# Operand pieces, accumulator loads and the rounding of w3 in a fused attention and expert kernel

## The chip, the cores and the metric

The kernel runs on one core of a Trainium2 chip. The metric is the device time of one execution in microseconds (us), as the median over runs. Before the change it is 1210.27 us (three runs, 1209.18 to 1212.36).

## The reference

An attention over pooled keys and values gives x (2304 tokens, 512 wide); four experts, weighted by domain probabilities, follow; then a gated block with four weights:

```python
def _moe_ref(x, domain_probs, w1, w2):          # 4 experts, 512 -> 1024 -> 512
    p = domain_probs / (domain_probs.sum(-1, keepdims=True) + 1e-09)
    for e in range(E):
        h = np.maximum(x @ w1[e], 0.0)
        out += p[:, e:e + 1] * (h @ w2[e])

def _moe2_ref(x, w1, w2, w3, w_out):            # 512 -> 1024 -> 1024 -> 512
    a = x @ w1
    b = x @ w2
    h = a * b @ w3
    return (h @ w_out).astype(np.float32)
```

Here q, k, v and the experts' weights are float32; the four weights of the gated block come as float64 words, and the kernel rounds them to float32 on the chip.

## The kernel before

Every matrix product is made of three float32r matmuls on high and low parts (`mm3`, L169). The order of the work is written out by hand: the program text is the order on each engine and each DMA queue.

**Stages.** Attention and expert 0 come first. Then experts e = 1, 2, 3 run over the four batches of 576 tokens (`batch`, L1134); during the end of expert 3 the product of w3 and w_out begins, and the gated block follows. The change lies in experts 1 to 3.

**One batch** has two stages. The first is four calls of `hidden` (L1115), j = 0 to 3, each one `seven` (L913): a scheme with seven products of sums of blocks in place of eight. A product is 6 matmuls of 288 columns (so 42 a seven, 168 a batch). It takes its bank from a ring of eight PSUM banks (`bank_r`, L163); VectorE adds it to others on line 919, ScalarE and GpSimd make the hidden rows z from it (`sink`). The second stage multiplies z with w2: T tiles of 128 tokens (T = 4 in even positions n, 5 in odd ones), each 8 x 3 matmuls of 512 columns in a bank of its own. A "place" is one step of three matmuls; there are 8 T places. In the first 6 T the tiles take turns; then each tile has its last two, and at its last place `give` (L1186) has VectorE compute bank times probability plus the accumulator piece `ob` (L1188), which frees the bank. The piece is then stored to DRAM (L1190); in expert 3 it is transposed (`turn`, L1177; the first three tiles at once, the others during the next batch's sevens) and written as `turned`.

**What is done at places of the second stage** is a table (`act`, L1167 to L1224). Before the change:
- `fetch_operand` (L779) loads the next batch's operands (7 blocks x 4 rows of 288, high and low, from `kept_x` to `xo`) in eight column pieces of 4032 B a partition, at places 0 to 7, on ScalarE's DMA queue. All seven blocks of a row lie side by side in a piece.
- `load_ob` (L1172) loads the accumulator pieces at places 14 (m < 3) and 10, on ScalarE's queue; in the last batch of an expert on SP's queue, the fifth at place 4 T + 5. The first three use the tiles `c`, which the sevens use for their sums.
- `round_some` runs steps of the rounding: 6, 8, 7 of them in the second stages of the batches n = 0, 1, 2 at places spread over 1 to 6 T - 3; one more step falls into each of the sevens j = 1 and 3 from n = 1 on.

**Rounding** (L229 to L286). `step` keeps three loads in flight (`load`, L243, on SP), computes with five or six VectorE instructions and one GpSimd addition, and one step later hands the result to a sink, which stores it. There are 80 steps: 16 of w_out, 32 of w3, 32 of the gate weights. So w_out falls into e = 1, n = 0 and 1; w3 into e = 1, n = 2 to e = 2, n = 2; the gates into the rest. A step of w3 (`rounded_T`, L301) takes 128 rows and 256 columns; VectorE transposes it in blocks of 32 x 32 into one of two `turned` buffers (L309), and four DMAs of 32 partitions, 256 runs of 128 B each, write it transposed (L312).

Every DMA issue on a queue waits in order for what its tile needs, and for one earlier DMA that used the same semaphore.

Of the kernel before, what the change touches and what calls it, by code (L numbers as in the profile page):

```python
# [17 lines left out]
def fused_kernel(  # L18
# [159 lines left out]
    class Stream:  # L178
# [55 lines left out]
    class Rounding:  # L234
# [66 lines left out]
    def rounded_T(src, name):  # L301
# [3 lines left out]
        d = dpool.tile([n, rows], F32, tag=name, name=name)  # L305

        def sink(t, i, c):
            tt = dec.tile([P, HALF], F32, tag="turned", name="turned")
            nc.vector.transpose(tt, t)  # L309
            for m in range(P // 32):  # L310
                to = d[c:c + HALF, i * P + 32 * m:i * P + 32 * (m + 1)]
                nc.sync.dma_start(to.rearrange("(b i) j -> i b j", i=32),  # L312
                                  tt[32 * m:32 * (m + 1)].rearrange("i (b j) -> i b j", j=32))

        for i in range(rows // P):
            for c in range(0, n, HALF):
                rounding.add(words[i * P:(i + 1) * P, 2 * c:2 * (c + HALF)], lambda t, i=i, c=c: sink(t, i, c), "turn")
        return d

    with tc.manual_schedule():  # L320
# [456 lines left out]
        PIECES = 4  # L777
# [52 lines left out]
        def enter_experts():  # L830
            nonlocal dec
            x5[:] = [area(f"x5{t}", XT, F32, "x5" + t) for t in "hl"]
            dec = Places(din=row(x5[0], 0, 2048, 3), store=row(x5[1], 0, 2048, 3), turn=row(x5[1], 0, 2048, 2), turned=row(x5[1], 4096, 1024, 2))
            xuv = dict(x=Ring(plain, [2 * XB + 6 * HALF_ROW]), u=Ring(plain, [2 * XB + 7 * HALF_ROW]), v=Ring(p_area, [3 * HALF_ROW]))
            areas["x1l"] = area("x1l", XT, F32R, "edge")
            late["small"] = Places(c=c_ring, s=row(plain, 0, 2 * ROW, 2), turned=row(plain, 0, ROW, 2) + Ring(plain, [3 * ROW]),
                                   ob3=Ring(p_area, [320]), ob4=Ring(plain, [2 * ROW]), last=row(plain, 0, ROW, 4) + Ring(p_area, [320]),
# [75 lines left out]
        def seven(j, sink, meanwhile=None):  # L913
# [145 lines left out]
        def stream_last():  # L1059
            def add_w3(n):  # L1060
                _, (b,), fc = w_units[n]
                t0, rn = w3_blocks[b]
                stream.add([late["w3"][fc * P:(fc + 1) * P, t0 * P:(t0 + rn) * P]], (1, rn * P), rn)

            for k, fc in enumerate(turn_of):
# [3 lines left out]
                stream.add([late["wo"][fc]], (1, DM), dst)  # L1069
# [45 lines left out]
        def hidden(j, b, meanwhile=None):  # L1115
# [9 lines left out]
            seven(j, sink, meanwhile)  # L1125
# [8 lines left out]
        def batch(e, n, b):  # L1134
            last, end = n == B - 1, n == B - 1 and e == E - 1
            small = late["small"]
            for j in range(NJ):
# [22 lines left out]
            begin = b * S + -(b * S) % P  # L1160
# [253 lines left out]
```

## Time and profile before

| | us |
|---|---|
| median of 3 runs | 1210.27 (1209.18 to 1212.36) |
| the profiled execution | 1213.8 |
| its span, first to last instruction | 1212.1 |
| TensorE busy | 1165.7 (96%) |
| VectorE busy | 802.8 (66%) |
| GpSimd busy | 486.5 (40%) |
| ScalarE busy | 378.2 (31%) |
| mean granted TensorE clock | 0.989 |
| DMA of SP's queue | 168.91 MB, 45.5% of 16 engines |
| DMA of ScalarE's queue | 47.39 MB, 11.4% of 16 engines |

PE is TensorE, DVE VectorE, ACT ScalarE, POOL GpSimd, SP the queue of SyncE; a q behind an engine means its sequencer, which waits and issues DMAs. A clock of 1.00 is 2.4 GHz, 0.50 is 1.2 GHz. L12 is line 12 of the kernel. Names of tiles stand as out<-in.

### The profile page before, as it was taken

The page shows a single profiled execution, that of the slowest core. Times are in us where ns is not written, and L with a number is a line of the kernel's source. Part 1 is how long each engine was busy: PE and PEld are TensorE (multiplying, and loading weights), DVE is VectorE, ACT ScalarE, POOL GpSimd, SP SyncE. Part 2 cuts the span into 40 slices and gives each one's busy share as a digit, 9 for nine tenths or more (in the row PEclk, how much of TensorE's full clock was granted, in tenths as well). Part 3 has the DMA queues.
Part 4 walks back from the last instruction along what each step waited for, and adds up shares of the span by engine and source line. Part 5 has one row for each costly group of instructions (what it writes and reads, how often), then busy time and mean ns, then how long its engine had stood idle before and what let it go on. Part 6 is the DMA issues. An engine that isn't in the chain of part 4 may idle for free.

```text
span 1212.1 us, 19303 instructions
## 1 busy us (share of the span) xinstructions
PE 1165.7 (96%) x6812; PEld 1051.6 (87%) x6812; DVE 802.8 (66%) x1623; ACT 378.2 (31%) x688; POOL 486.5 (40%) x569
## 2 busy tenths in 40 slices
PE   7999999999999989999879999998999999999998
PEld 5798888999888888988869888797888999999997
DVE  6776543566585676766758667676687777785454
ACT  4443432346122133421304433031544332331010
POOL 6875222267262447633426664352300222251121
PEclk9999999999999999999899999998999999999999
DMA  8765524454846755467583654848467244845651
GB/s 201 194 158 136 163 99 149 151 217 169 284 152 211 219 145 171 140 188 228 134 259 109 193 192 118 278 123 235 144 178 263 103 161 167 320 171 206 224 181 44
DMA packets 209936, 217.52 MB, mean 179 GB/s; under 512 B 92720, under 2 KB 152880, under 8 KB 209840
## 3 DMA queue, kind: packets, MB, share of 16 engines
q1 hardware_dynamic: 193856, 168.91, 45.5%
q10 hardware_dynamic: 15984, 47.39, 11.4%
q8 instruction: 53, 0.87, 0.3%
q14 instruction: 43, 0.35, 0.1%
HBM read 144.41 MB, written 71.83 MB: 178 GB/s over the span
## 4 chain that ended last, share of the span: by engine, by line
PE 36%; DMA 8%; DVE 5%; POOL 3%; issue 2%; ACT 1%; SPq 0%; DVEq 0%; ACTq 0%; POOLq 0%
PE s L170 7%; PE s L172 7%; PE s L171 7%; PE g L171 5%; PE g L172 5%; PE g L170 5%; DMA w<-x5l 3%; DMA gate<-x5l 2%; POOL round L176 2%; DVE plain L919 1%; DVE x5l L277 1%; DMA plain<-acc 1%; DMA xo<-keptx 1%; DMA x5h<-in_moe_w_dram 1%; DVE x5l L273 1%
## 5 line engine op out<-in xcount | busy, mean ns | idle before, releaser
L176 POOL TENSOR_TENSOR round<-plain,round 128x576 fp32r<-128x576 f32 (+1 forms) x131 | 189.5, 1447 | 399.5 <-ACT round L175 303.3
L170 PE MATMUL s<-xo,wh 128*128 128x288 f32 x840 | 253.6, 302 | 30.7 <-DVE plain L1188 28.7
L172 PE MATMUL s<-xo,wh 128*128 128x288 f32 x840 | 251.7, 300 | 0.0
L171 PE MATMUL s<-xo,wl 128*128 128x288 f32 x840 | 251.0, 299 | 0.0
L170 PE MATMUL g<-w2l,round 128*128 128x512 f32 x540 | 211.6, 392 | 0.0
L172 PE MATMUL g<-w2h,round 128*128 128x512 f32 x540 | 210.9, 391 | 0.0
L171 PE MATMUL g<-w2h,round 128*128 128x512 f32 x540 | 210.8, 390 | 0.1
L170 PEld LDWEIGHTS s<-xo,wh 128*128 128x128 f32 x840 | 161.4, 192 | 35.1 <-DVE plain L1188 29.5
L919 DVE TENSOR_TENSOR plain<-s,plain 128x288 f32<-128x288 f32 x320 | 135.5, 452 | 73.7 <-PE s L172 40.0
L171 PEld LDWEIGHTS s<-xo,wl 128*128 128x128 f32 x840 | 161.2, 192 | 0.7
L172 PEld LDWEIGHTS s<-xo,wh 128*128 128x128 f32 x840 | 161.3, 192 | 0.0
L175 ACT ACTIVATE round<-plain 128x576 fp32r<-128x576 f32 (+1 forms) x135 | 90.9, 676 | 162.0 <-DVE plain L1263 159.0
L1122 ACT ACTIVATE plain<-plain 128x576 f32<-128x576 f32 x96 | 65.4, 682 | 183.0 <-DVE plain L919 182.6
L172 PEld LDWEIGHTS g<-w2h,round 128*128 128x128 f32 x540 | 101.3, 188 | 21.4
L170 PEld LDWEIGHTS g<-w2l,round 128*128 128x128 f32 x540 | 101.5, 188 | 20.8 <-issue 0.8
L171 PEld LDWEIGHTS g<-w2h,round 128*128 128x128 f32 x540 | 101.4, 188 | 20.1 <-DVE round L660 0.4
L279 POOL TENSOR_TENSOR x5l<-x5l 128x256 uint32<-128x256 uint32 x80 | 59.0, 737 | 143.2 <-DVE x5l L278 132.8
L921 ACT ACTIVATE plain<-s 128x288 f32<-128x288 f32 x80 | 31.9, 399 | 229.6 <-DMA plain<-acc 109.8
L919 DVE TENSOR_TENSOR plain<-s,pb 128x288 f32<-128x288 f32 x160 | 68.2, 455 | 19.2 <-PE s L172 7.4
L660 DVE SCALAR_TENSOR_TENSOR round<-g,round 128x384 fp32r<-128x384 f32 x48 | 26.6, 553 | 68.7 <-ACT round L659 68.4
L273 DVE TENSOR_SCALAR x5l<-x5h 128x256 uint32<-128x256 uint32 x80 | 39.4, 493 | 44.1 <-DMA gate<-x5l 13.0
L170 PE MATMUL g<-xl,round 128*128 128x384 f32 x192 | 66.6, 347 | 0.0
(249 smaller groups left out, 2247.4 us busy)
## 6 DMA issues: line engine op xcount, KB each, us to landing
xo<-keptx ACTq DMA_DIRECT2D x72, 504.0 KB
raw<-in_moe_w_dram SPq DMA_DIRECT2D x64, 256.0 KB
x5h<-in_moe_w_dram SPq DMA_DIRECT2D x64, 256.0 KB
keptx<-xo SPq DMA_DIRECT2D x16, 576.0 KB
plain<-acc ACTq DMA_DIRECT2D x30, 256.0 KB
acc<-plain SPq DMA_DIRECT2D x28, 256.0 KB
kept<-xo SPq DMA_DIRECT2D x12, 576.0 KB
xo<-kept SPq DMA_DIRECT2D x10, 576.0 KB
```

Of the source, the lines that this page charges most:

```text
L170: nc.tensor.matmul(ps, lh, rl, start=first, stop=False)
L171: nc.tensor.matmul(ps, ll, rh, start=False, stop=False)
L172: nc.tensor.matmul(ps, lh, rh, start=False, stop=last)
L175: nc.scalar.activation(hi, src, AF.Copy)
L176: (lo_eng or nc.vector).tensor_tensor(lo, src, hi.bitcast(F32), op=ALU.subtract)
L273: nc.vector.tensor_scalar(au, h, 0x7FFFFFFF, None, op0=ALU.bitwise_and)
L277: nc.vector.scalar_tensor_tensor(au, au, 3, bu, op0=ALU.logical_shift_left, op1=ALU.bitwise_xor)
L279: nc.gpsimd.tensor_tensor(au, au, bu, op=ALU.add)
L660: nc.vector.scalar_tensor_tensor(hl, ps, 0.0, hh.bitcast(F32), op0=ALU.max, op1=ALU.subtract)
L919: nc.vector.tensor_tensor(to, one, two, op=ALU.add)
L921: nc.scalar.activation(x, product(j, A11, B11), AF.Copy)
L1122: nc.scalar.activation(r, r, AF.Relu)
```

## The change

1. Operands: one piece for each of the seven blocks, all rows, high and low (4 runs of 1152 B a partition), on SP's queue. The first four are issued in the seven j = 3, behind its third to sixth product, each after its block's last use there; the other three at places 2, 6 and 10.
2. Accumulator pieces: loaded behind the seven j = 1, on SP's queue, into places of their own; in the last batches of experts 1 and 2 at places 5 to 9. In expert 3 all tiles are turned at once, the first three into `c` tiles.
3. w3 is rounded 32 rows at a time: four loads of 32 rows x 256 columns fill the 128 partitions, the transposed result goes out in one DMA of 1024 runs of 128 B. There are four `turned` buffers. The columns then lie in another order, so the rows of w_out are loaded in that order, in four pieces of 32 rows.
4. The rounding's places: 3 to 6 T - 6 instead of 1 to 6 T - 3.

```diff
@@ Stream.fill
                 if isinstance(src, list):
+                    step = P * a // len(src)
                     for j, part in enumerate(src):
-                        nc.sync.dma_start(r[:, j, :], part)
+                        nc.sync.dma_start(r[j * step:(j + 1) * step, 0], part)
@@ Rounding.load
+                if src.shape[0] < P:
+                    for n in range(0, P, 32):
+                        nc.sync.dma_start(view[n:n + 32], src[n // 32])
+                    self.loaded.append((r, sink, tag))
+                    continue
@@ rounded_T
-        d = dpool.tile([n, rows], F32, tag=name, name=name)
-        def sink(t, i, c):
+        d = dpool.tile([n // P, P, rows], F32, tag=name, name=name)
+        def sink(t, r):
             tt = dec.tile([P, HALF], F32, tag="turned", name="turned")
             nc.vector.transpose(tt, t)
-            for m in range(P // 32):
-                to = d[c:c + HALF, i * P + 32 * m:i * P + 32 * (m + 1)]
-                nc.sync.dma_start(to.rearrange("(b i) j -> i b j", i=32),
-                                  tt[32 * m:32 * (m + 1)].rearrange("i (b j) -> i b j", j=32))
-        for i in range(rows // P):
-            for c in range(0, n, HALF):
-                rounding.add(words[i * P:(i + 1) * P, 2 * c:2 * (c + HALF)], lambda t, i=i, c=c: sink(t, i, c), "turn")
+            to = d[:, :, r:r + 32].rearrange("b p j -> p b j")
+            nc.sync.dma_start(to, tt.rearrange("p (b j) -> p b j", j=32))
+        for r in range(0, rows, 32):
+            rounding.add(words[r:r + 32].rearrange("j (q c) -> q j c", q=P // 32), lambda t, r=r: sink(t, r), "turn")
@@ operands
-        def fetch_operand(b, kc, n):
-            step = 2 * XO // 4 // PIECES
-            cols = slice(n * step, (n + 1) * step)
-            nc.scalar.dma_start(whole(kc)[:, cols], kept_x[b][:, kc].rearrange("p n a s -> p (n a s)")[:, cols])
-            xo_next[kc] = x_places[kc]
+        USED = [B11, T2, T3, T4, T1, B21, B22]
+        def fetch_operand(b, n):
+            m = USED[n]
+            there = late["xo"].bitcast(F32).rearrange("p (g m s) -> p g m s", m=7, s=HB)[:, :, m]
+            nc.sync.dma_start(there, kept_x[b].rearrange("p k n m s -> p (k n) m s")[:, :, m])
+            if n == 0:
+                xo_next.update(enumerate(x_places))
@@ enter_experts: dec gets turned=row(x5[1], 4096, 1024, 2) + Ring(plain, [4 * ROW]) + Ring(p_area, [320 + ROW])
-            late["small"] = Places(..., turned=row(plain, 0, ROW, 2) + Ring(plain, [3 * ROW]),
-                                   ob3=Ring(p_area, [320]), ob4=Ring(plain, [2 * ROW]), last=row(plain, 0, ROW, 4) + Ring(p_area, [320]),
+            late["small"] = Places(..., turned=row(plain, 0, ROW, 2),
+                                   ob0=Ring(plain, [0]), ob1=Ring(plain, [ROW]), ob2=Ring(plain, [2 * ROW]), ob3=Ring(p_area, [320]),
+                                   ob4=Ring(plain, [3 * ROW]), ob5=Ring(x5[1], [2 * ROW]),
@@ seven
             add(v, product(j, S3, T3), u)
+            behind(0)
             add(c1[:, 0], product(j, A22, T4), v)
+            behind(1)
             p5 = product(j, S1, T1)
             add(c1[:, 1], p5, v)
             add(u, p5, u)
             sink(1, c1, None)
+            behind(2)
             add(c0[:, 0], product(j, A12, B21), x)
+            behind(3)
             add(c0[:, 1], product(j, S4, B22), u)
@@ stream_last
-                stream.add([late["wo"][fc]], (1, DM), dst)
+                rows = [divmod(256 * q + 32 * fc, P) for q in range(P // 32)]
+                stream.add([late["wo"][i][at:at + 32] for i, at in rows], (1, DM), dst)
@@ batch
+            def load_ob(m):
+                tag = "c" if last and not end and m < 3 else f"ob{m}"
+                if tag == "ob4" and last and not end:
+                    tag = "ob5"
+                obs[m] = small.tile([P, DM], F32, tag=tag, name="ob")
+                nc.sync.dma_start(obs[m], acc_d[:, tiles[m][0]])
             for j in range(NJ):
-                if j in (0, 2) and pieces_late:
-                    some.append(pieces_late.pop(0))
-                hidden(j, b, lambda: [f() for f in some])
+                kw = dict(behind=lambda i: fetch_operand(orders[e][n + 1], i)) if j == NJ - 1 and not last else {}
+                hidden(j, b, meanwhile=lambda: [f() for f in some], **kw)
+                if j == 1 and (end or not last):
+                    for m in range(T):
+                        load_ob(m)
-                tag = "last" if end else "c" if m < 3 else f"ob{m}"
-                (nc.sync if last else nc.scalar).dma_start(obs[m], acc_d[:, tiles[m][0]])
-                tt = late["small"].tile([P, DM], F32, tag="turned", name="tt")
+                tt = late["small"].tile([P, DM], F32, tag="c" if m < 3 and not end else "turned", name="tt")
-                elif m < 3 and not end:
+                elif not end:
                     turn(m)
-            for m in range(T):
-                act(14 if m < 3 else 10 if m == 3 or not last else 4 * T + 5, lambda m=m: load_ob(m))
             if not last:
-                for i in range(2 * PIECES):
-                    act(i, lambda i=i: fetch_operand(orders[e][n + 1], i // PIECES, i % PIECES))
+                for i in range(4, 7):
+                    act(4 * i - 14, lambda i=i: fetch_operand(orders[e][n + 1], i))
                 some = 8 if n == 1 else 6 + n // 2
                 for i in range(some):
-                    act(1 + (6 * T - 4) * i // (some - 1), lambda: round_some(1))
+                    act(3 + (6 * T - 9) * i // (some - 1), lambda: round_some(1))
             elif not end:
+                rounding.flush()
+                for m in range(T):
+                    act(5 + m, lambda m=m: load_ob(m))
```

## Rows read from the trace of the kernel before

**Rows 1.** The page's first part: busy us, share of the span and instructions by engine.
```profile
PE 1165.7 (96%) x6812; PEld 1051.6 (87%) x6812; DVE 802.8 (66%) x1623; ACT 378.2 (31%) x688; POOL 486.5 (40%) x569
```

**Rows 2.** The view of waits, whole span: us in total, times, longest.
```profile
PE s L170 <- DVE plain L1188: 29.0, 11, 6.4
...
PE s L170 <- DVE pb L919: 1.1, 2, 0.6
...
DVE x5l L309 <- DMA w<-x5l: 17.7, 11, 4.5
```

**Rows 3.** Busy times by stretch: four sevens each; then clock, DMA share, GB/s.
```profile
322.48:345.94 23.46, 22.86 (x169) 22.39 (x168) 17.33 (x35) 9.21 (x16) 11.12 (x12) 1.00 0.37 123
...
373.16:399.59 26.43, 24.11 (x170) 23.88 (x168) 17.88 (x39) 9.30 (x16) 11.70 (x14) 0.94 0.38 126
...
421.36:450.29 28.93, 24.11 (x170) 23.87 (x168) 22.10 (x52) 9.21 (x16) 13.09 (x15) 0.94 0.61 164
...
477.50:501.89 24.39, 22.56 (x169) 22.35 (x168) 12.03 (x28) 12.12 (x22) 16.43 (x17) 1.00 0.36 113
...
523.67:547.93 24.26, 23.03 (x170) 22.39 (x168) 18.43 (x43) 9.20 (x16) 11.14 (x13) 1.00 0.48 129
...
575.14:604.74 29.60, 24.41 (x170) 24.17 (x168) 22.37 (x55) 9.44 (x16) 14.19 (x17) 0.88 0.51 138
...
626.52:657.83 31.31, 24.91 (x169) 24.68 (x168) 22.46 (x53) 9.44 (x16) 14.00 (x17) 0.89 0.55 164
...
685.05:707.39 22.34, 22.34 (x169) 22.34 (x168) 12.09 (x28) 11.62 (x22) 14.96 (x16) 1.00 0.35 116
...
729.17:753.76 24.59, 23.39 (x170) 22.45 (x168) 19.27 (x39) 9.21 (x16) 10.42 (x12) 1.00 0.44 102
...
780.98:806.77 25.79, 23.40 (x170) 22.47 (x168) 20.45 (x43) 9.21 (x16) 10.79 (x13) 1.00 0.54 124
...
828.74:859.11 30.37, 25.02 (x170) 24.78 (x168) 24.69 (x56) 9.85 (x17) 13.62 (x16) 0.89 0.67 182
```

**Rows 4.** TensorE and VectorE in order of time, around 421 to 430.
```profile
429.55 0.40 PE L170 MATMUL s<-xo,wh 128*128 128x288 f32 x1 [4.82 <-DVE plain L1188]
...
421.21 0.45 DVE L309 STREAM_TRANSPOSE x5l<-x5l 128x256 f32<-128x256 f32 x1 [4.47 <-DMA w<-x5l]
...
428.74 1.41 DVE L1188 SCALAR_TENSOR_TENSOR plain<-g,pb,plain 128x512 f32<-128x512 f32 x2
```

**Rows 5.** Busy times by stretch: one second stage; two sevens j = 3.
```profile
399.59:421.36 21.77, 21.77 (x98) 18.02 (x97) 13.12 (x33) 2.64 (x4) 7.06 (x9) 1.00 0.91 280
...
541.90:547.93 6.03, 6.03 (x48) 6.03 (x46) 5.06 (x13) 3.96 (x7) 5.57 (x7) 1.00 0.01 1
...
800.50:806.77 6.27, 6.27 (x50) 6.27 (x48) 5.35 (x13) 4.17 (x7) 5.42 (x7) 1.00 0.39 84
```

**Rows 6.** DMA queues: packets, MB, share; 399.59 to 429.5, then the whole span.
```profile
q10 hardware_dynamic: 1728, 5.18, 48.4%
q1 hardware_dynamic: 8229, 2.53, 40.8%
...
q1 hardware_dynamic: 193856, 168.91, 45.5%
```

**Rows 7.** DMA issues on SP: ns min, median, max by line; a spell in time.
```profile
L312 SPq DMA_DIRECT2D w<-x5l x128: 302/442/1759, 397.7 to 626.3; - x128
...
L447 SPq DMA_DIRECT2D stxh<-in_q_dram x36: 311/430/4413, 16.2 to 146.2; - x36
...
L435 SPq DMA_DIRECT2D stxl<-in_q_dram x1: 578/578/578, 3.3 to 3.3; - x1
...
415.23 6.22 SPq L312 DMA_DIRECT2D w<-x5l  x4
```

**Rows 8.** VectorE in order of time: the first instruction of two steps.
```profile
631.60 0.29 DVE L273 TENSOR_SCALAR x5l<-x5h 128x256 uint32<-128x256 uint32 x1
...
633.54 0.28 DVE L273 TENSOR_SCALAR x5l<-x5h 128x256 uint32<-128x256 uint32 x1
```

More of the change, by code (lines that the diff above doesn't have):

```diff
@@ L304, in rounded_T @@
         words = src.bitcast(U32)
[L305 to L307 removed]
+        d = dpool.tile([n // P, P, rows], F32, tag=name, name=name)
+        assert n == P // 32 * HALF
+        def sink(t, r):
             tt = dec.tile([P, HALF], F32, tag="turned", name="turned")
             nc.vector.transpose(tt, t)
[L310 to L317 removed]
+            to = d[:, :, r:r + 32].rearrange("b p j -> p b j")
+            nc.sync.dma_start(to, tt.rearrange("p (b j) -> p b j", j=32))
+        for r in range(0, rows, 32):
+            rounding.add(words[r:r + 32].rearrange("j (q c) -> q j c", q=P // 32), lambda t, r=r: sink(t, r), "turn")
         return d
@@ L832, in enter_experts @@
             x5[:] = [area(f"x5{t}", XT, F32, "x5" + t) for t in "hl"]
-            dec = Places(din=row(x5[0], 0, 2048, 3), store=row(x5[1], 0, 2048, 3), turn=row(x5[1], 0, 2048, 2), turned=row(x5[1], 4096, 1024, 2))
+            dec = Places(din=row(x5[0], 0, 2048, 3), store=row(x5[1], 0, 2048, 3), turn=row(x5[1], 0, 2048, 2), turned=row(x5[1], 4096, 1024, 2) + Ring(plain, [4 * ROW]) + Ring(p_area, [320 + ROW]))
             xuv = dict(x=Ring(plain, [2 * XB + 6 * HALF_ROW]), u=Ring(plain, [2 * XB + 7 * HALF_ROW]), v=Ring(p_area, [3 * HALF_ROW]))
             areas["x1l"] = area("x1l", XT, F32R, "edge")
-            late["small"] = Places(c=c_ring, s=row(plain, 0, 2 * ROW, 2), turned=row(plain, 0, ROW, 2) + Ring(plain, [3 * ROW]),
-                                   ob3=Ring(p_area, [320]), ob4=Ring(plain, [2 * ROW]), last=row(plain, 0, ROW, 4) + Ring(p_area, [320]),
+            late["small"] = Places(c=c_ring, s=row(plain, 0, 2 * ROW, 2), turned=row(plain, 0, ROW, 2),
+                                   ob0=Ring(plain, [0]), ob1=Ring(plain, [ROW]), ob2=Ring(plain, [2 * ROW]), ob3=Ring(p_area, [320]),
+                                   ob4=Ring(plain, [3 * ROW]), ob5=Ring(x5[1], [2 * ROW]),
                                    xr=Ring(x5[1], [0]), t=Ring(x5[0], [0]), **xuv)
@@ L911, in settle, with seven @@
                 pending.pop(0)()
-        def seven(j, sink, meanwhile=None):
+        def seven(j, sink, meanwhile=None, behind=lambda n: None):
             x, u, v = (late["small"].tile([P, HB], F32, tag=t, name=t, bufs=1) for t in "xuv")
@@ L1062, in add_w3 @@
                 t0, rn = w3_blocks[b]
-                stream.add([late["w3"][fc * P:(fc + 1) * P, t0 * P:(t0 + rn) * P]], (1, rn * P), rn)
+                stream.add([late["w3"][fc, :, t0 * P:(t0 + rn) * P]], (1, rn * P), rn)
             for k, fc in enumerate(turn_of):
@@ L1113, in take_x, with hidden @@
             xo_next.clear()
-        def hidden(j, b, meanwhile=None):
+        def hidden(j, b, **kw):
             at = (0, P - S % P) if b % 2 else (S - S % P, 0)
@@ L1124, in sink @@
                 nc.gpsimd.tensor_copy(edge_of(fc)[:, :, at[1]:at[1] + S % P], t[:, :, at[0]:at[0] + S % P])
-            seven(j, sink, meanwhile)
+            seven(j, sink, **kw)
         def round_some(n):
@@ L1136, in batch @@
             small = late["small"]
+            begin = b * S + -(b * S) % P
+            tiles = [(begin // P + m, lambda fc, off=begin - b * S + m * P: z_t[fc][:, :, off:off + P]) for m in range(S // P)]
+            if n % 2:
+                tiles.insert(0, ((b // 2 * 2 + 1) * S // P, edge_of))
+            T = len(tiles)
+            obs = {}
+            def load_ob(m):
[4 more added lines that the diff above has]
+                nc.sync.dma_start(obs[m], acc_d[:, tiles[m][0]])
             for j in range(NJ):
@@ L1159, in batch @@
                 stream.fill()
-            begin = b * S + -(b * S) % P
-            tiles = [(begin // P + m, lambda fc, off=begin - b * S + m * P: z_t[fc][:, :, off:off + P]) for m in range(S // P)]
-            if n % 2:
-                tiles.insert(0, ((b // 2 * 2 + 1) * S // P, edge_of))
-            T = len(tiles)
             banks = [bank_r("g2") for _ in tiles]
-            obs = {}
             acts = {}
@@ L1170, in act @@
                 acts.setdefault(at, []).append(f)
-            def load_ob(m):
-                tag = "last" if end else "c" if m < 3 else f"ob{m}"
-                obs[m] = small.tile([P, DM], F32, tag=tag, name="ob")
-                (nc.sync if last else nc.scalar).dma_start(obs[m], acc_d[:, tiles[m][0]])
             def turn(m):
                 t = tiles[m][0]
-                tt = late["small"].tile([P, DM], F32, tag="turned", name="tt")
+                tt = late["small"].tile([P, DM], F32, tag="c" if m < 3 and not end else "turned", name="tt")
                 nc.vector.transpose(tt, obs[m])
```

1 line of the change is left out of this document (removed).

## The prediction

> **What bounds the kernel now.** I read the first part of the page first. TensorE is busy for 1165.7 us, 96% of the span [rows 1], so no more than some 46 us can go unless matmuls go, and none go here. Next come the waits of TensorE: the one large entry is the first matmul of a product behind line 1188, 29.0 us in 11 waits [rows 2]. Line 1188 is the step in which VectorE adds a finished bank to the accumulator piece, and it is what frees the bank. Then I cut experts 1 to 3 into stages and asked for the busy times of each stretch of four sevens (168 matmuls) [rows 3]. The stretch from 685.05 is undisturbed and takes 22.34 us; the other ten rows are the same work. Their excess over 22.34 is 1.1, 4.1, 6.6, 2.1, 1.9, 7.3, 9.0, 2.3, 3.5 and 8.0 us, in sum **45.7 us**. It holds the idle time and, where the granted clock reads 0.94, 0.89 or 0.88, time at 1.2 instead of 2.4 GHz after it: 0.12 of 29.60 us is 3.6 us in the worst row. The second stages of the batches show no excess: 21.8 us with four tiles at clock 1.00 [rows 5], 27.2 with five (753.76 to 780.98, between two of the stretches) [rows 3]. So all that can be won lies in the first 3 to 9 us behind a batch boundary.
>
> Why does line 1188 come late? At one boundary (e = 1, third batch) TensorE finishes the second stage at 421.4, computes four products into the four free banks (to 424.7), and stands for 4.82 us. VectorE meanwhile waits 4.47 us in a transpose of the w3 rounding for a store, and only at 428.74 reaches the first line 1188 [rows 4]. Rounding steps stand before line 1188 in VectorE's order, so their transfers set the end. And the DMA engines are full there: from 399.59 to 429.5 the ACT queue (operands and accumulator pieces) took 48.4% and SP's queue (rounding) 40.8% of their time, 14.5 and 12.2 us out of 29.9 [rows 6]. In the last seven before a second stage they are nearly idle, 0.01 and 0.39 at two places, against 0.91 in a second stage [rows 5].
>
> **The change, part by part.** *Operands.* The bytes stay: 8 x 504 KB were 4.13 MB a batch, now 7 pieces of 590 KB, with runs of 1152 B in place of 4032 B. The ACT queue moved 5.18 MB in 14.5 us, 2.8 us per MB, so the operands cost 11.6 us of all DMA engines [rows 6]. For runs of 1152 B no row of this fetch exists. SP's queue over the whole span, mean packet 871 B, took 45.5% of 1212.1 us for 168.91 MB, 3.27 us per MB [rows 6], which gives 13.5 us; SP's queue in the busy window, mostly 128 B packets, took 12.2 us for 2.53 MB and would give 19.9 us. I take 13.5 us (871 B is nearest to 1152), 1.9 us a piece, and keep 11.6 and 19.9 as ends. Four pieces are now issued behind the third to sixth product of the last seven. Each waits for a product that TensorE has already left behind, and no transfer but the pieces stands behind it on SP until place 2 of the second stage. About 3.2 us of the seven remain, so 7.7 - 3.2 = 4.5 us of these transfers still run when the second stage begins. Three pieces, 5.8 us, follow at places 2, 6 and 10. They feed products 5 to 7 of the next seven, 20 us later.
>
> *Accumulator pieces.* Of the 14.5 us, 20% of the bytes (1.05 of 5.18 MB) are these, 2.9 us. They go to the second seven, where nothing waits for them, and out of the place right before line 1188. Their own wait, for the previous batch's stores, is over: these were issued a whole seven earlier. On SP only the transfers of later sevens stand behind them. In the last batch of experts 1 and 2 they come at places 5 to 9 instead of 10 to 25; this takes away the late fifth piece (2.1 us behind expert 1).
>
> *Rounding of w3.* The same 32 steps. On SP a step was one load and four stores, five issues at the stores' median of 0.44, 2.2 us [rows 7]. Now it is four loads of 32 rows and one store of 1024 runs. The nearest rows are the 32-row loads of q, 0.31 to 0.43 us, and a 1024-run load, 0.58 us [rows 7]: 1.8 to 2.3 us. No change, I say, and ends of -0.4 and +0.1 us a step. The step's DMA time I keep at 12.2 / 7 = 1.74 us, since bytes and 128 B runs stay. What goes is the wait for one of two turned buffers (now four). The Trainium skill (DMA: Bandwidth & Descriptors, Bandwidth) says that transfers under 64 KB are dominated by their descriptors and lists 0.95 us for 64 KB: stores of 128 instead of 32 KB would gain by it, while four loads at 0.95 would cost 3.8 us a step instead of the load's share in the 1.74 us. That estimate would put the w3 boundaries back where they are, the first rival below; no run of before shows a 64 KB load by itself.
>
> *The other edits* cost nothing on TensorE's path: w_out in four 32-row loads (24 more DMAs, near 10 us of SP's time, spread over 70 us in which TensorE is fed), and the turns of tiles 4 and 5 in expert 3, which move from the next sevens to line 1188's chain and cost 0.7 us each, under the cover of the free banks. The ACT queue loses 8 + 4 or 5 issues a batch; they lie beside other work.
>
> **The sum for one boundary.** With four tiles and seven w3 steps the DMA engines have 4.5 + 5.8 + 12.2 = 22.5 us of work in a second stage, against 26.7 before. Line 1188 hurts only if it comes later than 21.8 + 3.2 = 25.0 us. With five tiles and eight steps it is 4.5 + 5.8 + 13.9 = 24.2 against 27.2 + 2.4 = 29.6. VectorE's own pace, when nothing makes it wait, is 1.94 us a step [rows 8], 2.4 with the transpose: 7 steps from place 3 end at 2.0 + 16.7 = 18.7 us. All three are inside. So I expect the boundary waits to go and with them the low clock: -45.7 us. I put back 5: 1.1 us of waits behind line 919 that the change does not touch [rows 2], 0.5 us at each of four w3 boundaries, where the margin is 2.5 us, and 2 us for the turns in expert 3. The profiled execution took 1213.8 us, 3.5 above the median of the runs shown. 1213.8 - 45.7 + 5 = 1173.1 in its time, **1170 us** against the median. Only differences over 0.3% can be told from no change.
>
> **Rivals.** *The w3 boundaries stay (chance 0.18).* Operands and rounding now share one queue, and behind it a rounding load waits for whole operand pieces, 1.9 us each. With the upper price of a piece (19.9 / 7 = 2.84 us) the sum above is 8.2 + 8.5 + 12.2 = 28.9 us, 3.9 over the 25.0. For it speaks that the margin is thin; against it that the transposes' own waits for stores of w, 17.7 us in 11 [rows 2], were for one of two buffers and now have four. Then 6.6, 1.9, 7.3 and 9.0 us stay: 1164.6 + 24.8 = **1189 us**. The Trainium skill (DMA: Bandwidth & Descriptors, Queues, rings and completion order) has the DMA engines alternate between the queues that have work, which by itself speaks for this rival: on one queue there is no such turn. No run of before shows it apart.
>
> *SP becomes the bound (0.07), the slower case.* SP issues in order. A w3 step has five transfers, so a four-tile stage has 7 x 5 + 3 = 38. At 0.44 us each that is 17 us, but four stores in a full spell took 6.22 us, 1.55 us each, waits included [rows 7]. The point from which it decides is (25.0 - 2.0) / 38 = 0.6 us an issue. At 1.0, midway, SP ends 15 us late, with some 2.7 us of low clock after it; four such boundaries cost 71 us in place of 24.8, while the others still gain 21: 1210.3 + 46 - 21 = **1235 us**. Against it: SP had 28 of these stores and the loads in the window before, and issued most at 0.44.
>
> *No net change (0.03).* The last sevens have no room after all (the 0.39 in one of them), the operand pieces come late in place of line 1188: about **1210 us**.
>
> **How the numbers follow.** The forecast has 0.72: from 1163 (nothing put back, 1210.3 - 45.7 = 1164.6, less the spread of the runs) to 1178. The first rival runs from 1178 to 1200. A range from 1163 to 1191 holds the forecast and over half of the first rival, some 0.82. Faster: 0.72 + 0.18 = 0.90; same 0.03; slower 0.07.
>
> **What would show it.** Right: the ten stretches of four sevens at 22.3 to 23.5 us and clock 1.00, the wait behind line 1188 near zero, DMA share over 0.5 in the last sevens and lower in the second stages, no transpose waiting for a store of w. First rival: 24 to 31 us stays in the four stretches behind w3 stages alone. Second: SP's stores far over 0.6 us. The prediction is wrong if a stretch without w3 keeps its excess, or if TensorE waits for an operand piece.

## The result and the profile after

The median went from 1209.76 us (1209.18 to 1212.36, four runs) to **1167.44 us** (1165.97 to 1167.82, four runs): ratio 0.9644, 95% interval 0.9627 to 0.9661. The forecast was 1170, range 1163 to 1191. The profiled execution of the changed kernel took 1167.28 us, its span 1165.6.

The page's first part, which answers to [rows 1]: TensorE's share is now 99%.

```profile
PE 1151.6 (99%) x6812; PEld 1042.5 (89%) x6812; DVE 794.0 (68%) x1623; ACT 379.9 (33%) x688; POOL 486.8 (42%) x569
```

The view of waits, which answers to [rows 2] (line 1188 is now 1204, the transpose of line 309 is 316):

```profile
PE s L170 <- DVE plain L1204: 1.4, 1, 1.4
...
DVE x5l L279 <- DMA x5h<-in_moe_w_dram: 27.6, 13, 3.7
```

One wait of 29.0 us in 11 became one of 1.4. The waits of TensorE behind line 919 (now 925) are gone from the view. No transpose waits for a store any more; what VectorE waits for in the rounding is mostly its loads (27.6 us), and but for these 1.4 us that no longer reaches TensorE.

Busy times by stretch, which answer to [rows 3] and [rows 5]: four stretches of four sevens; then two sevens j = 3 (before a w3 stage, before a gate stage); then two second stages. The last three numbers are clock, DMA share and GB/s.

```profile
320.56:342.90 22.34, 22.34 (x170) 22.34 (x168) 18.71 (x42) 9.32 (x16) 12.71 (x15) 1.00 0.60 193
...
414.24:438.20 23.96, 22.56 (x169) 22.33 (x168) 20.97 (x49) 9.21 (x16) 12.41 (x14) 1.00 0.62 161
...
603.22:625.56 22.34, 22.34 (x169) 22.34 (x168) 18.01 (x40) 9.44 (x16) 12.75 (x15) 1.00 0.47 144
...
790.58:812.92 22.34, 22.34 (x169) 22.34 (x168) 17.92 (x38) 10.00 (x18) 11.25 (x13) 1.00 0.68 166
...
386.90:392.46 5.56, 5.56 (x45) 5.56 (x43) 4.00 (x10) 2.22 (x4) 4.29 (x6) 1.00 0.21 29
...
713.70:719.24 5.54, 5.54 (x43) 5.54 (x43) 3.96 (x9) 2.20 (x4) 4.22 (x6) 1.00 0.57 179
...
392.46:414.24 21.78, 21.78 (x99) 18.02 (x98) 12.61 (x36) 2.64 (x4) 7.50 (x10) 1.00 0.92 267
...
581.44:603.22 21.78, 21.78 (x98) 18.03 (x97) 15.55 (x43) 2.63 (x4) 8.24 (x11) 1.00 1.00 301
```

Ten of the eleven stretches take 22.34 us at clock 1.00; the one from 414.24 has 1.62 us over it. So 45.7 us of excess became 1.6. What did not change: the DMA engines are as full in the second stages as before (0.92 and 1.00, against 0.91 in [rows 5]).

VectorE and TensorE in order of time around the one wait left, which answers to [rows 4]:

```profile
414.24 0.29 DVE L279 TENSOR_SCALAR x5l<-x5h 128x256 uint32<-128x256 uint32 x1 [2.35 <-DMA x5h<-in_moe_w_dram]
...
418.20 2.06 DVE L1204 SCALAR_TENSOR_TENSOR plain<-g,pb,plain 128x512 f32<-128x512 f32 x3
...
419.00 0.40 PE L170 MATMUL s<-xo,wh 128*128 128x288 f32 x1 [1.40 <-DVE plain L1204]
```

SP's issues in order of time, ahead of that second stage:

```profile
390.25 0.39 SPq L318 DMA_DIRECT2D w<-x5l  x1
390.73 3.76 SPq L786 DMA_DIRECT2D xo<-keptx  x5
```

Line 1204 comes 4.0 us behind the second stage (418.20 - 414.24), where line 1188 came 7.4 us behind it (428.74 - 421.36). And the early operand pieces start at 390.73 only, 1.7 us before the second stage, since SP, which issues in order, stands before the rounding's store until 390.25.

The DMA queues, which answer to [rows 6], for 392.46 to 419 and for 393.2 to 396.2, where almost nothing but operand pieces moves:

```profile
q1 hardware_dynamic: 11095, 6.54, 88.2%
...
q1 hardware_dynamic: 1002, 1.12, 105.9%
```

Issues on SP by line (ns min, median, max), which answer to [rows 7]:

```profile
L318 SPq DMA_DIRECT2D w<-x5l x16: 366/385/408, 390.2 to 590.2; - x16
...
L251 SPq DMA_DIRECT2D x5h<-in_moe_w_dram x128: 310/419/1457, 359.8 to 585.9; - x128
```

88.2% of 26.54 us is 23.4 us of DMA time from the start of that stage to TensorE's restart; the sum had 22.5. Runs of 1152 B moved 1.12 MB in 3.0 us (3.2 by the packets' own time, 105.9%), 2.7 to 2.8 us per MB, 1.6 to 1.7 us a piece, where the sum took 1.9.

### The profile page after: what moved, and what is told of

The parts are those of the page before. It is cut to its first block, busy times and chain, and to the rows that moved or that the text cites. A ratio compares the mean times of both kernels' runs of the same rounds, so it can differ in the third digit from the quotient of the medians.

```text
span 1165.6 us, 19401 instructions
## 1 busy us (share of the span) xinstructions
PE 1151.6 (99%) x6812; PEld 1042.5 (89%) x6812; DVE 794.0 (68%) x1623; ACT 379.9 (33%) x688; POOL 486.8 (42%) x569
## 4 chain that ended last, share of the span: by engine, by line
PE 91%; DMA 2%; DVE 2%; POOL 2%; issue 1%; SPq 1%; ACT 1%; DVEq 0%; ACTq 0%; POOLq 0%
PE g L171 16%; PE g L172 16%; PE g L170 16%; PE s L170 13%; PE s L172 13%; PE s L171 13%; PE x_ps L525 1%; PE sc L479 1%; DMA xo<-keptx 1%; PE at_ps L513 1%; DMA plain<-in_v_dram 0%; DMA x5h<-in_moe_w_dram 0%; SPq L439 0%; POOL w2l L176 0%; POOL plain L809 0%
## 5 line engine op out<-in xcount | busy, mean ns | idle before, releaser
L170 PE MATMUL s<-xo,wh 128*128 128x288 f32 x840 | 248.4, 296 | 1.4 <-DVE plain L1204 1.4
L172 PE MATMUL s<-xo,wh 128*128 128x288 f32 x840 | 248.3, 296 | 0.0
L171 PE MATMUL s<-xo,wl 128*128 128x288 f32 x840 | 247.7, 295 | 0.0
L170 PEld LDWEIGHTS s<-xo,wh 128*128 128x128 f32 x840 | 158.0, 188 | 2.3 <-DVE plain L1204 1.6
L171 PEld LDWEIGHTS s<-xo,wl 128*128 128x128 f32 x840 | 157.7, 188 | 0.7
L172 PEld LDWEIGHTS s<-xo,wh 128*128 128x128 f32 x840 | 158.0, 188 | 0.0
L664 DVE SCALAR_TENSOR_TENSOR round<-g,round 128x384 fp32r<-128x384 f32 x48 | 26.6, 554 | 69.2 <-ACT round L663 69.0
L279 DVE TENSOR_SCALAR x5l<-x5h 128x256 uint32<-128x256 uint32 x80 | 37.2, 465 | 49.8 <-DMA x5h<-in_moe_w_dram 27.6
```

Of the source, the lines that this page charges most:

```text
L170: nc.tensor.matmul(ps, lh, rl, start=first, stop=False)
L171: nc.tensor.matmul(ps, ll, rh, start=False, stop=False)
L172: nc.tensor.matmul(ps, lh, rh, start=False, stop=last)
L279: nc.vector.tensor_scalar(au, h, 0x7FFFFFFF, None, op0=ALU.bitwise_and)
L664: nc.vector.scalar_tensor_tensor(hl, ps, 0.0, hh.bitcast(F32), op0=ALU.max, op1=ALU.subtract)
```

## The experiments

Each run was timed beside the kernel before on the same chip. Where a run is set against the changed kernel, the two were timed on different chips; the median of the kernel before lay between 1209.8 and 1212.3 us on them, so 2 us of such a difference say little. "Excess" is, as in the prediction, the duration of each stretch of four sevens less 22.34 us, from the busy times by stretch of each trace; the columns name the second stage in front of it by expert and batch (w: w_out rounded there, 3: w3, g: gates, L: an expert's last batch).

| kernel | us | ratio to before (95%) | 1.0 w | 1.1 w | 1.2 3 | 1.3 L | 2.0 3 | 2.1 3 | 2.2 3g | 2.3 L | 3.0 g | 3.1 g | 3.2 g | sum |
|---|---|---|---|---|---|---|---|---|---|---|---|---|---|---|
| before | 1209.8 | 1 | 1.1 | 4.1 | 6.6 | 2.1 | 1.9 | 7.3 | 9.0 | 0 | 2.3 | 3.5 | 8.0 | 45.7 |
| after | 1167.4 | 0.9644 (0.9627, 0.9661) | 0 | 0 | 1.6 | 0 | 0 | 0 | 0 | 0 | 0 | 0 | 0 | 1.6 |
| undo_obs | 1189.3 | 0.9827 (0.9794, 0.9861) | 0 | 0 | 6.7 | 0.5 | 0 | 1.4 | 5.6 | 3.6 | 0 | 0.5 | 6.4 | 24.6 |
| undo_ops | 1182.7 | 0.9770 (0.9741, 0.9800) | 0 | 0 | 1.4 | 0 | 0 | 1.3 | 7.1 | 0 | 0 | 0 | 5.5 | 15.2 |
| undo_w3 | 1172.9 | 0.9691 (0.9659, 0.9724) | 0 | 0 | 1.6 | 0 | 0 | 0 | 6.8 | 0 | 0 | 0 | 0 | 8.4 |
| only_obs | 1184.9 | 0.9793 (0.9765, 0.9821) | 0 | 0 | 4.1 | 0 | 0 | 0.3 | 7.5 | 0 | 0 | 0 | 5.5 | 17.4 |
| only_ops | 1191.7 | 0.9844 (0.9818, 0.9870) | 0 | 0 | 5.4 | 1.5 | 0 | 2.1 | 9.9 | 0.6 | 0 | 0 | 5.8 | 25.3 |
| only_w3 | 1206.7 | 0.9979 (0.9964, 0.9994) | 0 | 4.7 | 8.1 | 1.2 | 0.2 | 7.5 | 6.0 | 1.8 | 2.2 | 5.1 | 5.2 | 42.0 |
| double_pieces | 1266.5 | 1.0469 (1.0445, 1.0493) | 11.0 | 7.0 | 15.3 | 0 | 9.5 | 13.0 | 15.5 | 0 | 7.8 | 7.6 | 13.6 | 100.1 |
| ops_on_act | 1169.6 | 0.9672 (0.9652, 0.9692) | 0 | 0 | 0 | 0 | 0 | 0 | 0 | 0 | 0 | 0 | 3.8 | 3.8 |
| extra_copy | 1188.4 | 0.9824 (0.9801, 0.9847) | 4.4 | 0 | 6.9 | 0 | 0 | 5.7 | 2.6 | 0 | 0 | 0 | 2.5 | 22.1 |
| obs_first | 1178.5 | 0.9736 (0.9705, 0.9766) | 0 | 0 | 7.0 | 0 | 0 | 4.4 | 1.8 | 0 | 0 | 0 | 0 | 13.2 |
| round_j2 | 1166.4 | 0.9643 (0.9621, 0.9665) | 1.5 | 0 | 0 | 0 | 0 | 0 | 0 | 0 | 0 | 0 | 0 | 1.5 |
| split_queue | 1165.7 | 0.9639 (0.9616, 0.9661) | 0 | 0 | 0 | 0 | 0 | 0 | 0 | 0 | 0 | 0 | 0 | 0 |

The excess explains the times: each profiled execution's time less its sum lies between 1164.5 and 1168.1 us. But one trace's boundary also varies: up to the end of the first batch of expert 1 the programs of the changed kernel and of round_j2 are the same, and line 1204 comes 1.0 us behind that stage in the one (321.56) and 3.2 us in the other (322.56, the stage ends at 319.37). So 1 or 2 us at one boundary of one trace show nothing by themselves.

### One part undone

**undo_obs**, the accumulator pieces:

```diff
-                nc.sync.dma_start(obs[m], acc_d[:, tiles[m][0]])
+                (nc.sync if last else nc.scalar).dma_start(obs[m], acc_d[:, tiles[m][0]])
...
-                if j == 1 and (end or not last):
+                if j == 1 and end:
...
             if not last:
+                for m in range(T):
+                    act(14 if m < 3 else 10, lambda m=m: load_ob(m))
...
-                    act(5 + m, lambda m=m: load_ob(m))
+                    act(14 if m < 3 else 10 if m == 3 else 4 * T + 5, lambda m=m: load_ob(m))
```

> The changed kernel with the accumulator pieces loaded where they were: places 14 and 10 of the second stage on the ACT queue (own places in SBUF kept). Theory (the boundary waits come from the DMA time that lies ahead of VectorE's line 1188 in a second stage; a boundary waits only when this is more than its margin): 2.9 us more per second stage, of which the boundary with a margin of -0.6 us pays all and those with 2 to 3 us a little: 1172 to 1182 us, the stretch at 414 worst, gate stretches near 22.3. Rival (the pieces' own late landing was the wait nearly everywhere): 1195 us or more, with line 1188 waiting for DMA plain<-acc at most boundaries.

Measured 1189.3, 21.9 us over the changed kernel: between the two. Of the 24.6 us of excess 22.3 lie in four stretches, three behind third batches (6.7, 5.6, 6.4) and one behind expert 2's last; three more have 0.5 to 1.4. In the view of waits line 1204 does not wait for the pieces in the ordinary batches, so the rival's mechanism is not there; VectorE waits for rounding loads and gate stores. The theory's size was too small by 7 us or more. In the last batches the fifth piece at place 4 T + 5 has a wait of its own: the last row below is expert 2's (3.6 us), and in expert 1 (0.5 us) the fifth line 1204 is late too, 5.1 us behind its stage, though the view does not put that wait down to the piece:

```profile
DVE x5l L279 <- DMA x5h<-in_moe_w_dram: 44.9, 13, 6.8
...
DVE x5l L279 <- DMA gate<-x5l: 18.9, 9, 8.8
...
DVE x5l L1204 <- DMA x5l<-acc: 7.1, 1, 7.1
```

**undo_ops**, the operands (`fetch_operand` as it was, no `behind`):

```diff
-                kw = dict(behind=lambda i: fetch_operand(orders[e][n + 1], i)) if j == NJ - 1 and not last else {}
+                kw = {}
...
-                for i in range(4, 7):
-                    act(4 * i - 14, lambda i=i: fetch_operand(orders[e][n + 1], i))
+                for i in range(2 * PIECES):
+                    act(i, lambda i=i: fetch_operand(orders[e][n + 1], i // PIECES, i % PIECES))
```

> The changed kernel with the operands fetched as before: eight column pieces of 4032 B runs, places 0 to 7, ACT queue. Theory (DMA time in the second stage): only 1 to 3 us of the operands really ran in the last seven, so 1 to 3 us more a second stage: 1168 to 1178 us. Rival (the operands' place is the main term, as the prediction's sum has it with its 4.5 + 5.8 against 11.6 us): 1180 us or more.

Measured 1182.7: 15.2 us, above the theory's range, in the rival's, but nearly all in two stretches (7.1 and 5.5), both behind third batches. In the first of them TensorE waits for an operand, the second row (3.6 us), the wait that the prediction's third rival named; in the second VectorE waits for a store of the gates (9.2 us, shown further down):

```profile
PE s L170 <- DVE plain L1203: 5.3, 4, 2.8
PE s L170 <- DMA xo<-keptx: 3.8, 2, 3.6
```

**undo_w3**, the rounding of w3 (`rounded_T` and the loads of w_out as they were, two turned buffers; the places of the rounding stay):

```diff
...
-            to = d[:, :, r:r + 32].rearrange("b p j -> p b j")
-            nc.sync.dma_start(to, tt.rearrange("p (b j) -> p b j", j=32))
...
-        for r in range(0, rows, 32):
+            for m in range(P // 32):
+                to = d[c:c + HALF, i * P + 32 * m:i * P + 32 * (m + 1)]
+                nc.sync.dma_start(to.rearrange("(b i) j -> i b j", i=32), tt[32 * m:32 * (m + 1)].rearrange("i (b j) -> i b j", j=32))
+        for i in range(rows // P):
...
-    turned=row(x5[1], 4096, 1024, 2) + Ring(plain, [4 * ROW]) + Ring(p_area, [320 + ROW])
+    turned=row(x5[1], 4096, 1024, 2)
```

> The changed kernel with w3 rounded as before: 128 rows a step, four stores of 32 KB, two turned buffers. Theory: only the four stretches behind w3 stages can move, by the waits of the transposes for stores: 1170 to 1182 us. Rival (the w3 rounding was the cause, the rest only moved with it): the four stretches get their 24.8 us back, 1190 us or more. Rival (the bytes are the same, so nothing): within 1 us of 1167.4.

Measured 1172.9: 5.4 us, in the theory's range, and all of it in one of the four w3 stretches (2.2). Both rivals fall.

### One part alone

These three start from the kernel before, with places of their own for the accumulator pieces and expert 3's turns done at once; **only_obs** has their early load, **only_ops** the operand pieces, **only_w3** the rounding of w3. As edits of the changed kernel, each is the other two diffs above together with the rounding's old places:

```diff
-                    act(3 + (6 * T - 9) * i // (some - 1), lambda: round_some(1))
+                    act(1 + (6 * T - 4) * i // (some - 1), lambda: round_some(1))
```

> The kernel before with only the accumulator pieces moved to the second seven (and expert 3's turns done at once); operands, w3 and the places of the rounding as before. Theory: 2.9 us less in front of line 1188 at ten boundaries, each gaining at most that or its whole excess, plus clock: 45.7 us fall by 20 to 28, 1182 to 1190 us. Rival (this part alone is the gain): under 1173 us. Rival (rounding's transfers set the end, the pieces come after them anyway): over 1200 us.

> The kernel before with only the operands fetched by block on SP's queue, four in the last seven (and expert 3's turns done at once); accumulator pieces at places 14 and 10 on the ACT queue, w3 and the places of the rounding as before. Theory as the first four runs leave it (two chains end at line 1188: at most boundaries the accumulator pieces' own landing, behind w3 and in third batches the rounding): the pieces are no longer issued behind eight operand pieces on the ACT queue, but still land behind the full DMA engines: 1190 to 1200 us. Theory of the prediction (DMA time in the second stage, 11.6 us falls to 5.8 + 4.5 or less): 1.5 to 3 us a boundary, 1185 to 1197 us. Rival (moving this part alone helps nothing while the pieces are late): over 1205 us.

> The kernel before with only the rounding of w3 changed (32 rows a step, one store, four turned buffers; and expert 3's turns done at once). Theory: boundaries not behind w3 keep their waits for the accumulator pieces; those behind w3 gain 0 to 4 us each, since the pieces still come last: 1199 to 1208 us. Rival (w3's stores were the root): four stretches fall by 24.8 us, under 1190 us.

Measured, against the kernel before on the same chip: 1184.9 against 1212.3, 1191.7 against 1210.2, 1206.7 against 1210.2: -27.5, -18.5 and -3.5 us, the last of them only 0.3%. All three lie in the theory's ranges (only_ops in that of the prediction's theory too, so it doesn't tell these two apart). Added up they are -49.5, the three undone cost 21.9 + 15.2 + 5.4 = 42.5, and the whole change brought 42.3: the parts add up nearly, with some paid twice. The rounding's new places and the edits that all three share were not tried by themselves.

The accumulator pieces are the largest part. Moved alone, they leave 0.3 us or less at seven of the ten boundaries, with operands and w3 as before. They did harm in two ways, which the kernel before shows boundary by boundary. Line 1188 itself waited for them six times, up to 7.2 us (first row: the whole view; then VectorE in order of time at boundaries 1.1 and 3.0):

```profile
DVE plain L1188 <- DMA plain<-acc: 28.6, 6, 7.2
...
377.25 1.41 DVE L1188 SCALAR_TENSOR_TENSOR plain<-g,pb,plain 128x512 f32<-128x512 f32 x2 [6.34 <-DMA plain<-acc]
...
731.14 0.75 DVE L1188 SCALAR_TENSOR_TENSOR plain<-g,pb,plain 128x512 f32<-128x512 f32 x1 [7.19 <-DMA plain<-acc]
```

At 1.1, 1.3, 3.0 and 3.1 this wait is the last one before line 1188. These four have 12.0 us of the excess, and in only_obs all of it is gone. At 1.2, 2.0, 2.1, 2.2 and 3.2, with 32.8 us, a wait of the rounding stands last, as at 421. There only_obs takes away 15.4 us, on average 3.1 a boundary (1.5 to 7.0), about the 2.9 us of DMA time that the sum gave the pieces.

The first way needs the operands as well: in only_ops the pieces have their old places and queue but no operand pieces ahead of them, and line 1205 (1188 before) waits only for the fifth piece of last batches (first row). In only_w3 the operands stay ahead of them, and its line waits nine times (second row):

```profile
DVE x5l L1205 <- DMA x5l<-acc: 12.2, 2, 6.6
```

```profile
DVE plain L1203 <- DMA plain<-acc: 39.6, 9, 8.3
```

### DMA time against waits on SP

**double_pieces** and **extra_copy** move the same extra 1.77 MB in each second stage on SP's queue. The first loads each of the three operand pieces twice to the same place; the second copies the block to a scratch in DRAM that nothing reads:

```diff
                 for i in range(4, 7):
-                    act(4 * i - 14, lambda i=i: fetch_operand(orders[e][n + 1], i))
+                    for _ in range(2):
+                        act(4 * i - 14, lambda i=i: fetch_operand(orders[e][n + 1], i))
```

```diff
+        dump = [dpool.tile([P, 4, HB], F32, tag=f"dump{n}", name="dump") for n in range(27)]
+        def copy_operand(b, n):
+            nc.sync.dma_start(dump.pop(), kept_x[b].rearrange("p k n m s -> p (k n) m s")[:, :, USED[n]])
...
                 for i in range(4, 7):
                     act(4 * i - 14, lambda i=i: fetch_operand(orders[e][n + 1], i))
+                    act(4 * i - 14, lambda i=i: copy_operand(orders[e][n + 1], i))
```

> The changed kernel with the three operand pieces of the second stage loaded twice (same bytes to the same place; 1.77 MB more a second stage, nothing computed from the second copy that is not already there). Theory (DMA time in the second stage counts, whatever moves): at 2.7 us per MB the rounding ends 4.8 us later; margins left in the changed kernel are -0.6, 2.4, 2.8, 2.8 us where it is thin and over 5 elsewhere, so the stretches at 414, 320, 559 and 603 pay some 5, 2.4, 2 and 2 us, with clock 1176 to 1186 us. Rival (only the order of issue and the pieces' own landing count, the engines had room): under 1171 us.

> The changed kernel with three more transfers in each second stage: beside each of the three operand pieces the same block is copied from DRAM to a scratch in DRAM, issued on SP's queue, 0.59 MB each, and nothing waits for it or is written twice (double_pieces made SP wait for the first copy to land; this one has no such wait). Theory (DMA time in the second stage counts, whatever it moves): 1.77 MB at 2.7 us per MB is 4.8 us before line 1188; the stretches at 414, 320, 559 and 603 pay some 5, 2.4, 2 and 2 us and with clock 1176 to 1190 us. Rival (the engines have room, only waits on SP count): under 1171 us.

extra_copy: 1188.4, 20.9 us more, within the theory's range; its four thin stretches have 4.4, 6.9, 5.7 and 2.6 us, and 3.2, which the theory had not named, 2.5. So transfers in the second stage count, and where the margin is thin about at the 4.8 us put in. That SP would not wait for a copy was expected and is not quite so: it did in 12 places, 12.9 us in all, 1.3 at most. Its first row is

```profile
SPq L251 <- DMA dump<-keptx: 9.5, 9, 1.3
```

The copies also stand ahead of the rounding's loads on SP's queue, and no run has them on the other queue; so time of the engines and place in the queue are not told apart.

double_pieces: 1266.5, **99 us** more, which neither theory had. The extra copy must not overtake the first, so SP waits for the first to land, with the rounding's loads and stores queued behind it:

```profile
SPq L786 <- DMA xo<-keptx: 152.6, 28, 7.9
```

28 waits, 5.5 us each. Same bytes, queue and places (but to SBUF, where extra_copy writes to DRAM): 21 us with short waits, 99 with these. As a measurement of DMA time double_pieces is spoilt; it shows what a held-up SP costs, which the prediction's slower case had for another reason, slow issues.

**obs_first** puts the pieces back into the second stage, but first in line on SP:

```diff
-                if j == 1 and (end or not last):
+                if j == 1 and end:
...
             if not last:
+                for m in range(T):
+                    act(m, lambda m=m: load_ob(m))
```

> The changed kernel with the accumulator pieces loaded in the second stage again, but on SP's queue at its first places 0 to 4, so that they land long before line 1188. Theory (their 2.9 us of DMA time delay the rounding's loads): the same as with them at places 14 and 10, 1180 to 1192 us, and VectorE waits for rounding loads. Rival (their own late landing or the ACT queue was the cost): under 1173 us.

Measured 1178.5, a little under the theory's range, above the rival's: 11.1 of undo_obs's 21.9 us. Of the other 10.8, 4.1 us are the last batches, which this run leaves alone. The remaining 7 us came with places 10 and 14 and the ACT queue; which of the two isn't separated. Nor does the cost move evenly: obs_first has 4.4 us at 2.1, where undo_obs has 1.4, and none at 3.2, where undo_obs has 6.4.

### The queue and the order on SP

**round_j2** does a rounding step in j = 2 in place of j = 3; **ops_on_act** issues the new pieces on the ACT queue; **split_queue** does so for experts 1 and 2 only:

```diff
-                if j in (1, 3) and n:
+                if j in (1, 2) and n:
```

```diff
-            nc.sync.dma_start(there, kept_x[b].rearrange("p k n m s -> p (k n) m s")[:, :, m])
+            nc.scalar.dma_start(there, kept_x[b].rearrange("p k n m s -> p (k n) m s")[:, :, m])
```

```diff
...
-            nc.sync.dma_start(there, kept_x[b].rearrange("p k n m s -> p (k n) m s")[:, :, m])
+            (nc.scalar if e < E - 1 else nc.sync).dma_start(there, kept_x[b].rearrange("p k n m s -> p (k n) m s")[:, :, m])
```

> The changed kernel with the rounding step of the seven j = 3 done in j = 2. Theory (in front of w3 stages the four early operand pieces stand on SP behind that step's store, so they start some 2 us late): DMA share in the last seven of w3 batches rises from 0.21 to 0.5 or more, the wait at 414 falls under 0.5 us, 1165 to 1167 us. Rival (the wait at 414 has another cause): the same wait, 1167.4 us.

> The changed kernel with the seven operand pieces issued on the ACT queue in place of SP's, at the same points of the program. Theory of one queue in order (a rounding load waits behind whole pieces; and on SP the pieces wait behind a rounding store): the pieces start up to 2 us earlier in the last seven and the loads no longer queue behind them, the wait left at 414 goes: 1164 to 1167 us. Rival (the engines' time counts, not the queue): within 1 us of 1167.4 with the wait at 414 between 1 and 2 us. Rival (ScalarE's own work waits behind issues, as in the kernel before): 1172 us or more.

> The changed kernel with the operand pieces on the ACT queue in experts 1 and 2 and on SP's in expert 3. Theory (on the ACT queue the loads of w3 no longer queue behind pieces, while in expert 3's third batch the stores of the gates suffer from a second queue): no wait at 414 and none at the last boundary of expert 3, 1164 to 1167 us. Rival (the wait at the last boundary was chance): as the ACT queue for all, 1169.5 us.

round_j2: the DMA share of the last seven goes from 0.21 to 0.60 and the wait at 414 is gone, as expected:

```profile
386.70:392.30 5.60, 5.60 (x45) 5.60 (x44) 4.49 (x11) 2.93 (x5) 3.17 (x5) 1.00 0.60 167
...
414.57:436.91 22.34, 22.34 (x169) 22.34 (x168) 19.10 (x43) 9.21 (x16) 11.21 (x13) 1.00 0.59 156
```

Its 1.5 us of excess stands behind the first batch of expert 1, and most of it ahead of the first step that the edit moves; it is like the spread between executions named under the table. Its 1166.4 us are within the noise of the changed kernel's 1167.4. ops_on_act: the wait at 414 goes too, but the last gate boundary takes 3.8 us, so 1169.6 and not the 1164 to 1167 expected. split_queue: no excess at all, 1165.7 us (1165.4 to 1166.5). That is 0.15% under the changed kernel, less than a measurement tells apart; its trace alone says that it is better.

## Why the prediction was right, and where its steps were not

**The size and its ceiling held.** The ten excess stretches were the whole of what could be won: 45.7 us, of which 44.1 went. The time is 2.6 us under the forecast mainly because of the 5 us put back: the 1.1 us behind line 919, the turns in expert 3 and three of the four w3 boundaries cost nothing, 1.6 us stayed. They stayed where the sum had its thinnest margin, behind a four-tile stage with seven w3 steps (22.5 of 25.0 us estimated, 23.4 measured). Of the 3.5 us that the forecast took off, from the profiled execution of before to the median, a part lies ahead of the boundaries: the first seven of expert 1 starts at 278.4 us there, and between 275.3 and 278.3 in the other thirteen traces. One reading was off: in the stretch from 575.14 the low clock cost 24.41 - 22.34 = 2.1 us of busy time [rows 3], not 3.6; the rest of its 7.3 us is TensorE's wait. That changes no sum.

**"Rounding steps stand before line 1188, so their transfers set the end" was read from one boundary and holds at five of ten.** I followed the wait at 421 and took it for all ten. It holds for 32.8 of the 45.7 us. At four boundaries (12.0 us) line 1188's own wait for the accumulator pieces came last; it stood in the same view, 28.6 us in six waits, and was left unread. The 1.1 us at 1.0 begin with a wait of TensorE for an operand piece, 0.5 us. The number came out because the change also moved the pieces, and the sum let every boundary go to zero whatever held it: for these four that is luck. obs_first shows that the pieces, early in the stage and on SP, still cost about half of what their old place cost the changed kernel; whether as DMA time or by standing ahead of the rounding's loads isn't shown.

**"Four pieces run in the last seven" failed in front of w3.** "No transfer but the pieces stands behind it" looked behind the pieces and not ahead of them: the rounding's store stands in front of them on SP. The share there was 0.21 to 0.23, not over 0.5 (0.57 in front of gate stages, as forecast). So seven pieces at 1.6 to 1.7 us, 11.2 to 11.7 less at most 1.2 in the last seven, ran in the second stage; the sum's 4.5 + 5.8 = 10.3 is near that because its price per piece was too high and its early start too good: two errors that cancel, luck again. And the forecast "lower in the second stages" is wrong: 0.92 after 0.91. What fell at 414 is the DMA time up to TensorE's restart, 23.4 of 26.5 us where it was 26.7 of 29.9; extra_copy shows that a few us more are paid there.

**Terms.** A piece cost 1.6 to 1.7 us (taken: 1.9), a store of 1024 runs 0.38 us to issue (0.58), a 32-row load 0.42 (0.31 to 0.43). The Trainium skill (DMA: Bandwidth & Descriptors, Bandwidth) lists 0.95 us for a load of 64 KB, over 128 partitions and issued from GpSimd. The estimate made from it, 3.8 us for the four loads of a step, gives 26.6 us for seven steps; the stage measured 23.4 us of DMA time for everything in it. The trace does not agree with adding up that figure for these loads. Split or not, they cost the same: undo_w3, with seven loads of 256 KB in place of 28 of 64 KB, has 23.3 us in the same window (87.7% of 26.57, from 392.69 to 419.26):

```profile
q1 hardware_dynamic: 11781, 6.61, 87.7%
```

**The rivals.** None came true as a whole. The first (w3 boundaries stay) is right in one of four, with 1.6 of its 24.8 us. Its mechanism is there, only smaller than the margins: on SP the rounding's loads wait behind whole operand pieces,

```profile
SPq L251 <- DMA xo<-keptx: 13.0, 11, 2.3
```

and with the pieces on the ACT queue (ops_on_act) that row is gone, and the wait at 414 with it (single traces: 1.6 us in the changed kernel and in undo_w3, none in ops_on_act, round_j2 and split_queue). The Trainium skill's rule that the DMA engines alternate between queues (DMA: Bandwidth & Descriptors, Queues, rings and completion order) agrees with that; but a step moved on one queue (round_j2, which keeps that row at 13.2 us) takes the wait at 414 away as well, and with two queues another boundary waits, so no run here shows that the alternation does it. The slower case did not occur: the changed kernel's SP issues its stores, pieces and 32-row loads in 0.38 to 0.54 us (medians).

## What to carry to other kernels

Where an in-order engine holds the instruction that frees a buffer, list everything that it waits for, at every boundary, and not at the worst one alone: here two different waits came last at different boundaries, and the cheaper transfer (2.9 us of DMA time a stage) was worth the most since it came last in line at four of them and lay in the way of the rounding at others. A prefetch belongs where its queue is empty, and the queue must be read ahead of it as well as behind it: one store that waits for VectorE held back the early pieces by 2 us. A DMA that must wait long on an in-order queue can cost far more than its bytes: 99 us against 21 here.

## What the runs showed that I had not expected

VectorE's longest wait for a store of the gates mostly goes with a second queue: the row of the view of waits reads, for the changed kernel, split_queue (pieces on the ACT queue in experts 1 and 2 alone), ops_on_act and undo_ops (operands on the ACT queue throughout):

```profile
DVE x5l L279 <- DMA gate<-x5l: 7.5, 6, 2.1
```

```profile
DVE x5l L279 <- DMA gate<-x5l: 9.9, 6, 3.5
```

```profile
DVE x5l L279 <- DMA gate<-x5l: 16.5, 6, 7.2
```

```profile
DVE x5l L279 <- DMA gate<-x5l: 19.8, 7, 9.2
```

Up to 3.5 us with one queue in expert 3, 7 to 9 us with large loads on the ACT queue beside it. Most other traces fit (2.2 to 2.9 us in undo_w3, obs_first and round_j2; 8.0 to 9.0 in undo_obs, only_ops and only_obs), but not all: only_w3 has operands and accumulator pieces on the ACT queue and 4.0 us at most. So a second queue alone isn't shown to be the cause: in ops_on_act three of the accumulator pieces of that batch also were issued late, in the second stage (from 767.74 on), so the run changes two things at once. The time before expert 1 varies by up to 3 us from run to run; a difference of that size in one profile says nothing.
